# First rows of x loaded untransposed and interleaved with the blocks of wkA, five warm-ups for seven, in a gated pair of linear-attention blocks

## The chip, the cores and the metric

One core of a Trainium2 chip. The metric is the device time of one execution in microseconds (us). The kernel before takes 185.69 us, the median of three runs (185.13 to 186.56).

## The reference

Two linear-attention blocks A and B work on the same x, and a gate made from x mixes their outputs. S is 2048 rows, D is 640, with 32 heads of 20; all tensors are bf16.

```python
def block(x, wqkv, wo):
    q, k, v = heads(x @ wqkv)                      # 32 heads of 20
    phi = lambda t: where(t > 0, t + 1, exp(t)) + 1e-6
    pq, pk = phi(q), phi(k)
    kv  = einsum("bhsd,bhse->bhde", pk, v)
    z   = pk.sum over s
    num = einsum("bhqd,bhde->bhqe", pq, kv)
    den = einsum("bhqd,bhd->bhq", pq, z) + 1e-6
    return merge(num / den) @ wo

g = sigmoid((x * gate_w).sum(-1))
out = g * block(x, A_wqkv, A_wo) + (1 - g) * block(x, B_wqkv, B_wo)
```

## The kernel before

TensorE (PE) multiplies matrices, VectorE (DVE) and ScalarE (ACT) do the element-wise work out of PSUM, GpSimd (POOL) sets up small constants, and SyncE (SP) and ACT issue transfers, each on a queue of its own. In the parts under `manual_schedule`, `k_first` among them, the order of instructions on each engine is the order of the code; elsewhere a scheduler places them.

Work on the 2048 rows goes in 16 chunks of 128. A chunk of k is made by ten products (`k_mm`, L220): five blocks c of the inner dimension 640, and two halves hf of the 640 outputs. The left side is the transposed x (`xT`, five blocks of 128 by 2048), the right side the k part of the weights (`wkA`, five blocks). A 321st column in the second half of block A's weights holds `gate_w`, so that the same products give the gate's logit. `k_done` then makes `phi`: exp on ACT (L207), the logit's copy on ACT (L226), two steps on DVE (L212, L216).

`xT` has two sources. Rows 0 to 255 are loaded as they are into `xn` (L116) and transposed on PE against the identity (`x_transpose`, L199, five transposes per 128 rows), then copied from PSUM by DVE (L202). The other rows come by transposing loads on SP's queue (`x_turned`, L119): rows 256 to 511 first, then three times 512 rows. The loads of the start stand on two queues: SP has x's block 0, wkA's blocks 0, 2 and 4, the transposing load of rows 256 to 511, the whole of wqA (L132), and the other transposing loads; ACT has `gate_w`, x's block 1, and wkA's blocks 1 and 3.

While they are under way PE runs seven warm-up products on constants (L159), each 128x512, whose result is used by nobody. Then it turns `gate_w` into a column (L161), DVE copies the column, and POOL spreads it over wkA's extra column (L165). `k_first` transposes x's blocks 0 and 1, does the products of chunks 0 and 1 on blocks 0 to 2 in turn, then blocks 3 and 4, and then chunks 2 and 3 as wholes.

After that the first q products follow (`q_block` L278, `q_single` L288): for 512 rows at a time, with wqA as the left side. `q_block` fills two PSUM banks, one after the other, each with the five blocks c. PSUM has four slots of two banks (`ps`), which go round in a fixed order: chunks 0 to 3 have slots 2, 3, 0 and 1, and the first `q_block` has slot 2 again, so it waits until DVE is done with chunk 0. Later parts of the kernel are k, q, the sums over rows (Strassen products, L347), the same for block B, and at the end the output products (L570), which are added up by DVE (L575) and stored (L589).

Transfers carry one of eight semaphores in rotation, in the order of the code over both queues. A transfer waits until the one that had its semaphore before has landed. After its last transfer SP works down a list of waits, one for each semaphore, in the order 3 and 2, 4 and 1, 5 and 0, 6, 7, and then the program ends.

Of the kernel before, what the change touches and what calls it, by code (L numbers as in the profile page):

```python
# [8 lines left out]
P = 128  # L9
FP32 = mybir.dt.float32  # L10
BF16 = mybir.dt.bfloat16
# [3 lines left out]
S, D, H = 2048, 640, 32  # L15
Dh = D // H
DT = D // P
ST = S // P
NB = 4
CB = 4  # L20
HB = 512
# [10 lines left out]
def kernel(  # L32
# [11 lines left out]
    nc = tc.nc  # L44
# [6 lines left out]
    work = ctx.enter_context(tc.tile_pool(name="work", bufs=2))  # L51
# [6 lines left out]
    def ps_raw(name, slot=None):  # L58

        if slot is None:  # L60
            slot = turn[0]
            turn[0] = (slot + 1) % 4
        return psum.tile([P, 4 * HB], BF16, tag=f"ps{slot}", name=name)

    def ps(name, slot=None):

        return ps_raw(name, slot).bitcast(FP32).rearrange("p (b n) -> p b n", b=2)

    xT = persist.tile([P, DT, S], BF16, name="xT")
# [6 lines left out]
    ident = persist.tile([P, P], BF16, name="ident")  # L76
# [27 lines left out]
    wq_dram = [A_wqkv.rearrange("(c p) f -> p c f", p=P), B_wqkv.rearrange("(c p) f -> p c f", p=P)]  # L104
# [6 lines left out]
    wk = [None, None]  # L111
    wv = [None, None]
    wq = [None, None]
    wk[0] = wpool.tile([P, DT, D + 16], BF16, tag="wk", name="wkA")
    def load_x(eng, i):
        eng.dma_start(out=xn[:, i, :], in_=x2[i * P:(i + 1) * P, :])  # L116

    def x_turned(lo, hi):
        nc.sync.dma_start_transpose(out=xT[:, :, lo:hi], in_=x2[lo:hi, :])  # L119

    def load_wk(eng, lo, hi):
        eng.dma_start(out=wk[0][:, lo:hi, 0:D], in_=wq_dram[0][:, lo:hi, D:2 * D])

    grow = R[0][0:DT, 0:P]
    nc.scalar.dma_start(out=grow, in_=gate_w.rearrange("(c p) -> c p", p=P))
    load_x(nc.sync, 0)
    load_x(nc.scalar, 1)
    for c, eng in enumerate((nc.sync, nc.scalar, nc.sync, nc.scalar, nc.sync)):
        load_wk(eng, c, c + 1)
    x_turned(2 * P, HB)  # L130
    wq[0] = wpool.tile([P, DT, D], BF16, tag="wq", name="wqA")
    nc.sync.dma_start(out=wq[0][:], in_=wq_dram[0][:, :, 0:D])  # L132
    for n in range(1, NB):
        x_turned(n * HB, (n + 1) * HB)


    make_identity(nc, ident[:])
# [4 lines left out]
    for sign, base in ((1, 0), (-1, Dh - 1)):  # L142
        nc.gpsimd.affine_select(
            out=maskE[:], in_=maskE[:], pattern=[[-sign * Dh, WB[0] // Dh], [0, Dh]],
# [3 lines left out]
    for sign, base in ((1, 0), (-1, TW - 1)):  # L148
        nc.gpsimd.affine_select(
            out=headE[:], in_=headE[:], pattern=[[-sign * TW, H]],  # L150
# [4 lines left out]
    raw = ps_raw("warm", 3)  # L155
    warm = raw.bitcast(FP32).rearrange("p (b n) -> p b n", b=2)
    one_l, one_r = [nc.const_aps.tensor(1.0, [P, n], BF16) for n in (P, HB)]
    for k in range(7):
        nc.tensor.matmul(warm[:, 0, :], lhsT=one_l, rhs=one_r, start=True, stop=True)  # L159
    gcol = raw[:, 2 * HB:2 * HB + DT]  # L160
    nc.tensor.transpose(out=gcol, in_=grow, identity=ident[0:DT, 0:DT])  # L161
    gsb = work.tile([P, DT], BF16, tag="rT", name="gsb")
    nc.vector.tensor_copy(out=gsb[:], in_=gcol)
    for c in range(DT):
        nc.gpsimd.tensor_copy(out=wk[0][:, c, D:D + 1], in_=gsb[:, c:c + 1])  # L165

    def by_group(dst, lhsT, src, h):

# [28 lines left out]
    def x_transpose(i, pt, cuts=(0, DT)):  # L197
        for c in range(DT):
            nc.tensor.transpose(out=pt[:, c * P:(c + 1) * P], in_=xn[:, i, c * P:(c + 1) * P], identity=ident[:])  # L199
        src = pt[:, 0:D].rearrange("p (c n) -> p c n", c=DT)  # L200
        for lo, hi in zip(cuts, cuts[1:]):
            nc.vector.tensor_copy(out=xT[:, lo:hi, i * P:(i + 1) * P], in_=src[:, lo:hi])  # L202

    def phi(dst, src, n, lifted=False, side=None):

        e = work.tile([P, src.shape[1], n], BF16, tag="e", name="e", bufs=3)
        nc.scalar.activation(out=e[:], in_=src, func=ACT.Exp)  # L207
        if side is not None:
            side()
        if lifted:  # L210
            nc.scalar.activation(out=dst, in_=src, func=ACT.Identity, bias=lift[:])
        nc.vector.tensor_scalar(e[:], e[:], 1.0, EPS, op0=ALU.min, op1=ALU.add)  # L212
        if lifted:
            nc.vector.tensor_tensor(out=dst, in0=dst, in1=e[:], op=ALU.max)
            return
        nc.vector.scalar_tensor_tensor(out=dst, in0=src, scalar=1.0 + EPS, in1=e[:], op0=ALU.add, op1=ALU.max)  # L216

    def k_mm(b, i, c, pt, hf):
        w = HF + (hf if b == 0 else 0)
        nc.tensor.matmul(  # L220
            pt[:, hf, 0:w], lhsT=xT[:, c, i * P:(i + 1) * P], rhs=wk[b][:, c, hf * HF:hf * HF + w],
            start=(c == 0), stop=(c == DT - 1),
        )

    def k_done(b, i, pt):
        side = (lambda: nc.scalar.copy(out=logit[:, i:i + 1], in_=pt[:, 1, HF:HF + 1])) if b == 0 else None  # L226
        phi(pk[:, i, :].rearrange("p (b n) -> p b n", b=2), pt[:, :, 0:HF], HF, side=side)

    def k_chunk(b, i, slot=None):
        pt = ps(f"k{'AB'[b]}", slot)  # L230
        for hf in range(2):
            for c in range(DT):
                k_mm(b, i, c, pt, hf)
        k_done(b, i, pt)

    def k_first():

        pts = [ps("kA", 2 + i) for i in range(2)]
        raw = [ps_raw("xt", i) for i in range(2)]
        for i in range(2):  # L240
            x_transpose(i, raw[i], (0, 2, DT))

        def part(i, cs):
            for c in cs:
                for hf in range(2):
                    k_mm(0, i, c, pts[i], hf)

        for c in range(3):
            for i in range(2):
                part(i, (c,))  # L250
        for i in range(2):
            part(i, (3, 4))
            k_done(0, i, pts[i])
        for i in range(2, CB):
            k_chunk(0, i, i - 2)

    def mixed(t, m):

        return t[:, m::DT]
# [13 lines left out]
    def q_block(b, m, n):  # L273

        pt = ps(f"q{'AB'[b]}")
        for u in range(2):
            for c in range(DT):
                nc.tensor.matmul(  # L278
                    pt[:, u, :], lhsT=mixed(wq[b][:, c, :], m + u), rhs=xT[:, c, n * HB:(n + 1) * HB],
                    start=(c == 0), stop=(c == DT - 1),  # L280
                )
        phi(pqT[b][:, m:m + 2, n * HB:(n + 1) * HB], pt, HB)

    def q_single(b, m, n):
# [67 lines left out]
    def g_strassen(b, rT):  # L352
# [30 lines left out]
        if b == 0:  # L383
            wq[1] = load_w(1, "q", nc.scalar)
# [143 lines left out]
    part = [slice(n * RB, (n + 1) * RB) for n in range(4)]  # L528
# [113 lines left out]
                out_add(self.rows(0)[:, HF + lo:HF + hi], dst, self.v[:, lo:hi])  # L642
            self.store(0, HF if self.last else 0, D)

    def load_w(b, which, eng):
        lo = {"q": 0, "k": D, "v": 2 * D}[which]
        t = wpool.tile([P, DT, D], BF16, tag="w" + which, name=f"w{which}{'AB'[b]}")
        eng.dma_start(out=t[:], in_=wq_dram[b][:, :, lo:lo + D])
        return t

    def load_wo(b, eng):
        t = wo_sb[b] = wpool.tile([P, NW, D], BF16, tag="wo", name=f"wo{'AB'[b]}")
        for hf in range(2):
            for i, n in ((0, 2), (2, 1)):
                w, d0 = WB[i], hf * HF + i * WB[0]
                eng.dma_start(
                    out=t[:w, 3 * hf + i:3 * hf + i + n, :],
                    in_=wo_dram[b][d0:d0 + n * w, :].rearrange("(j p) f -> p j f", p=w),
                )
# [14 lines left out]


    with tc.manual_schedule():
        k_first()
    turn[0] = 2
    for n in range(2):
        for i in range(CB if n else 0, CB * 2 * n):  # L680
            k_chunk(0, i)
        for m in (0, 2):
            q_block(0, m, n)
        q_single(0, DT - 1, n)
    for i in range(hc, ST - 2):
        k_chunk(0, i)
    for n in range(NB):
        lo, hi = max(n * CB, 2), (n + 1) * CB
        nc.sync.dma_start(
            out=xn[:, lo:hi, :], in_=x2[lo * P:hi * P, :].rearrange("(q p) d -> p q d", p=P)  # L690
        )
    wv[0] = load_w(0, "v", nc.sync)
    load_wo(0, nc.sync)
    wk[1] = load_w(1, "k", nc.sync)

    def late_pool(name):
        return tc.tile_pool(name=name, bufs=1, space=bass.MemoryType.PSUM, reuse_waits="tile")
# [4 lines left out]
    with tc.manual_schedule():  # L702
# [17 lines left out]
        t = wpool.tile([P, 2, hc, HF], BF16, tag="wo", name="T13")  # L720
# [7 lines left out]
        t = wpool.tile([P, 2, DT, HF], BF16, tag="wq", name="TM12")  # L728
# [67 lines left out]
        for i in range(half - 1):  # L796
            p, after = pairs[i:i + 2]
# [45 lines left out]
```

## Time and profile before

| What | Value |
|---|---|
| median of three runs | 185.69 us |
| profiled execution | 186.37 us |
| its span, first to last instruction | 184.6 us |
| PE busy | 180.3 us, 98% of the span |
| DVE busy | 149.8 us, 81% |
| ACT busy | 75.1 us, 41% |
| bytes moved | 19.17 MB, mean 104 GB/s |

How to read it: "busy" counts the time in which an engine has an instruction at work; an L and a number is a line of the kernel. The span leaves out 1.77 us of the profiled execution that lie around the first and the last instruction. The chain of waits is followed back from the last instruction, at each step to what released it. A timeline line gives start, length, engine, line, operation, output <- inputs, sizes and count, and in brackets the idle time of the engine before it and what ended this. SPq and ACTq are the instructions that issue transfers. PE's matmuls are pipelined, so the sum of lengths can be longer than the time from the first to the last.

### The profile page before, as it was taken

What the parts mean: (1) busy time and instruction counts of PE and PEld (TensorE: products, weight loads), DVE (VectorE), ACT (ScalarE), POOL (GpSimd) and SP (SyncE); (2) the same over time, 40 slices, a digit from 0 to 9 for tenths busy, and PEclk for the clock granted to TensorE, in tenths of its full rate; (3) what the DMA queues carried; (4) which work ended last, traced back from release to release, by engine and by line L of the source; (5) the groups of instructions that cost most, each with busy time, mean ns of one, the idle gap of its engine ahead of it and who ended that gap; (6) DMA issues with size and microseconds to landing.
All of it is one profiled execution on the core that took longest, in us unless ns stands there. A gap on an engine that the chain in (4) does not pass through costs nothing.

```text
span 184.6 us, 3335 instructions
## 1 busy us (share of the span) xinstructions
PE 180.3 (98%) x1317; PEld 121.2 (66%) x1317; DVE 149.8 (81%) x239; ACT 75.1 (41%) x128; POOL 3.3 (2%) x22
## 2 busy tenths in 40 slices
PE   8999999999999999999999999999999999999993
PEld 3565757765567777877775555577778777777772
DVE  0286868889999999778788999779799999877873
ACT  2055545547962101357674577531102863111010
POOL 6000000000000000000000000000000000000000
PEclk9999999999999999999999999999999999999999
DMA  5999999124100270241115000000234570133333
GB/s 148 245 262 178 275 377 263 37 34 147 57 0 4 85 234 4 42 169 37 55 33 196 9 0 0 0 4 14 91 118 99 154 201 4 37 108 107 110 108 107
DMA packets 22518, 19.17 MB, mean 104 GB/s; under 512 B 10214, under 2 KB 21734, under 8 KB 22502
## 3 DMA queue, kind: packets, MB, share of 16 engines
q1 hardware_dynamic: 20564, 16.82, 33.6%
q10 hardware_dynamic: 1938, 2.13, 3.6%
q8 instruction: 10, 0.16, 0.4%
q14 instruction: 6, 0.05, 0.1%
HBM read 12.13 MB, written 4.53 MB: 90 GB/s over the span
## 4 chain that ended last, share of the span: by engine, by line
PE 94%; DMA 3%; ACTq 1%; DVE 0%; issue 0%
PE gs L347 17%; PE ox L570 12%; PE kB L220 12%; PE qB L267 12%; PE kA L220 12%; PE qA L267 6%; PE oz L570 6%; PE qA L278 5%; DMA wkA<-in_A_wqkv_dram 3%; PE gB L319 2%; PE gA L319 2%; PE ow L570 2%; PE qA L288 1%; PE s L474 1%; PE mA L474 1%; PE kvA L444 1%
## 5 line engine op out<-in xcount | busy, mean ns | idle before, releaser
L220 PEld LDWEIGHTS <-xT 128*128 128x128 bf16 x320 | 31.3, 98 | 13.2 <-issue 0.6
L212 DVE TENSOR_SCALAR e<-e 128x640 bf16<-128x640 bf16 (+2 forms) x53 | 19.0, 358 | 10.9 <-ACT e L207 9.7
L220 PE MATMUL kA<-wkA,xT 128*128 128x320 bf16 (+1 forms) x160 | 23.1, 304 | 0.2 <-DMA wkA<-in_A_wqkv_dram 0.2
L220 PE MATMUL kB<-wkB,xT 128*128 128x320 bf16 x160 | 23.0, 299 | 0.0
L267 PE MATMUL qB<-xT,wqB 128*128 128x512 bf16 x100 | 21.8, 379 | 0.0
L207 ACT ACTIVATE e<-kB 128x640 bf16<-128x640 f32 x16 | 11.3, 703 | 18.8 <-PE kB L220 18.8
L267 PEld LDWEIGHTS <-wqB 128*128 128x128 bf16 x100 | 11.7, 117 | 9.8 <-issue 0.2
L207 ACT ACTIVATE e<-kA 128x640 bf16<-128x640 f32 x16 | 11.2, 705 | 13.5 <-PE kA L220 13.5
L216 DVE SCALAR_TENSOR_TENSOR pk<-kA,e 128x640 bf16<-128x640 f32 x16 | 13.2, 825 | 2.1 <-DVE e L212 0.2
L216 DVE SCALAR_TENSOR_TENSOR pk<-kB,e 128x640 bf16<-128x640 f32 x16 | 13.2, 825 | 1.7
L207 ACT ACTIVATE e<-qB 128x1024 bf16<-128x1024 f32 x10 | 10.2, 1023 | 8.7 <-PE qB L267 8.3
L207 ACT ACTIVATE e<-qA 128x1024 bf16<-128x1024 f32 (+1 forms) x11 | 10.4, 946 | 8.1 <-PE qA L278 5.1
L347 PEld LDWEIGHTS <-xn 128*128 128x128 bf16 x96 | 9.2, 98 | 3.9 <-issue 0.4
L347 PEld LDWEIGHTS <-S 128*128 128x128 bf16 x96 | 9.4, 98 | 3.6
L620 ACT COPY u<-ox 128x320 f32<-128x320 f32 x8 | 3.4, 425 | 20.5 <-PE ox L570 20.5
L267 PE MATMUL qA<-xT,wqA 128*128 128x512 bf16 x50 | 11.0, 379 | 0.0
L570 PEld LDWEIGHTS <-xT 128*128 128x128 bf16 x85 | 8.1, 98 | 2.9
L570 PEld LDWEIGHTS <-pqTB 128*128 128x128 bf16 x80 | 7.8, 98 | 3.2
L570 PEld LDWEIGHTS <-pqTA 128*128 128x128 bf16 x80 | 7.7, 98 | 3.0
L347 PE MATMUL gs<-pk,xn 128*128 128x320 bf16 x64 | 9.4, 299 | 0.0
L216 DVE SCALAR_TENSOR_TENSOR pqTB<-qB,e 128x1024 bf16<-128x1024 f32 x7 | 8.6, 1225 | 0.7
L267 PEld LDWEIGHTS <-wqA 128*128 128x128 bf16 x50 | 5.9, 117 | 4.8
(126 smaller groups left out, 278.6 us busy)
## 6 DMA issues: line engine op xcount, KB each, us to landing
out_dram<-pk SPq DMA_DIRECT2D x14, 160.0 KB, 1.9
xn<-in_A_x_dram SPq DMA_DIRECT2D x3, 640.0 KB, 5.2
wqA<-in_A_wqkv_dram SPq DMA_DIRECT2D x1, 800.0 KB, 7.0
wvA<-in_A_wqkv_dram SPq DMA_DIRECT2D x1, 800.0 KB, 10.0
wkB<-in_B_wqkv_dram SPq DMA_DIRECT2D x1, 800.0 KB, 4.8
wqB<-in_B_wqkv_dram ACTq DMA_DIRECT2D x1, 800.0 KB, 5.2
wvB<-in_B_wqkv_dram SPq DMA_DIRECT2D x1, 800.0 KB
MA<-mA_dram SPq DMA_DIRECT2D x1, 800.0 KB, 4.2
```

What stands on the lines that cost most here:

```text
L207: nc.scalar.activation(out=e[:], in_=src, func=ACT.Exp)
L212: nc.vector.tensor_scalar(e[:], e[:], 1.0, EPS, op0=ALU.min, op1=ALU.add)
L216: nc.vector.scalar_tensor_tensor(out=dst, in0=src, scalar=1.0 + EPS, in1=e[:], op0=ALU.add, op1=ALU.max)
L220: nc.tensor.matmul(pt[:, hf, 0:w], lhsT=xT[:, c, i * P:(i + 1) * P], rhs=wk[b][:, c, hf * HF:hf * HF + w], start=(c == 0), stop=(c == DT - 1),
L267: nc.tensor.matmul(pt[:, u, :], lhsT=mixed(wq[b][:, c, :], m), rhs=xT[:, c, n * HB:(n + 1) * HB], start=(c == 0), stop=(c == DT - 1),)
L278: nc.tensor.matmul(pt[:, u, :], lhsT=mixed(wq[b][:, c, :], m + u), rhs=xT[:, c, n * HB:(n + 1) * HB], start=(c == 0), stop=(c == DT - 1),)
L288: nc.tensor.matmul(pt[:, 0, :], lhsT=mixed(wq[b][:, c, :], m), rhs=xT[:, c, n * HB:(n + 1) * HB], start=(c == 0), stop=(c == DT - 1),)
L319: nc.tensor.matmul(pt[:, hf, 0:HF], lhsT=xn[:, i, c * P:(c + 1) * P], rhs=pk[:, i, hf * HF:(hf + 1) * HF], start=(i == 0), stop=(i == ST - 1),
L347: nc.tensor.matmul(pt[:, n, 0:HF], lhsT=left[:, i, n * P:(n + 1) * P], rhs=right[:, i, :], start=(first and i == 0), stop=(i == hc - 1), s ...
L474: nc.tensor.matmul(dst[:w, 0:HF], lhsT=KVA[:w, k, 0:w], rhs=wo_sb[b][:w, k, n * HF:(n + 1) * HF], start=True, stop=True,)
L570: nc.tensor.matmul(dst, lhsT=left[:, c, r0:r0 + P], rhs=right[:, c, :], start=(first and c == 0), stop=(c == DT - 1), skip_group_check=not ...
L620: nc.scalar.copy(out=self.u6[:], in_=self.at("x"))
```

## The change

The first four blocks of x (rows 0 to 511) are now all loaded untransposed and turned on PE; the transposing load of rows 256 to 511 is gone, and so is the later load of these two blocks into `xn`. The loads of the start stand in a new order: ACT has x's block 1 first and `gate_w` after it; SP has everything else, the blocks of x and of wkA in turn. wqA comes in three pieces, wvA and wkB in two each.

On PE, five warm-ups are left, and the column of the gate is made between the transposes of x's blocks 0 and 1, with ACT and not DVE copying it. `k_first` then has: chunks 0 and 1 on wkA's blocks 0 and 1; transposes of x's block 2; chunks 0 and 1 on wkA's block 2; chunk 2 on blocks 0 to 2; transposes of x's block 3; blocks 3 and 4 for chunks 0, 1 and 2, each with its `phi`; chunk 3 as a whole. Inside a part the half hf is now the outer loop. `q_block` runs over the blocks c outside and the two banks inside. There are six more transfers on SP and two fewer on ACT, so the rotation of semaphores shifts by four: the last store has number 7 and not number 3, and the three stores before it have 6, 5 and 4 and not 2, 1 and 0.

```diff
-    nc.scalar.dma_start(out=grow, in_=gate_w.rearrange("(c p) -> c p", p=P))
-    load_x(nc.sync, 0)
-    load_x(nc.scalar, 1)
-    for c, eng in enumerate((nc.sync, nc.scalar, nc.sync, nc.scalar, nc.sync)):
-        load_wk(eng, c, c + 1)
-    x_turned(2 * P, HB)
     wq[0] = wpool.tile([P, DT, D], BF16, tag="wq", name="wqA")
-    nc.sync.dma_start(out=wq[0][:], in_=wq_dram[0][:, :, 0:D])
-    for n in range(1, NB):
-        x_turned(n * HB, (n + 1) * HB)
+
+    def first_loads():
+
+        load_x(nc.sync, 0)
+        load_x(nc.scalar, 1)
+        nc.scalar.dma_start(out=grow, in_=gate_w.rearrange("(c p) -> c p", p=P))
+        load_wk(nc.sync, 0, 1)
+        load_wk(nc.sync, 1, 2)
+        load_x(nc.sync, 2)
+        load_wk(nc.sync, 2, 3)
+        load_wk(nc.sync, 3, 4)
+        load_x(nc.sync, 3)
+        load_wk(nc.sync, 4, DT)
+        for lo, hi in ((0, 2), (2, 4), (4, DT)):
+            nc.sync.dma_start(out=wq[0][:, lo:hi, :], in_=wq_dram[0][:, lo:hi, 0:D])
+        for n in range(1, NB):
+            x_turned(n * HB, (n + 1) * HB)
...
-    for k in range(7):
-        nc.tensor.matmul(warm[:, 0, :], lhsT=one_l, rhs=one_r, start=True, stop=True)
-    gcol = raw[:, 2 * HB:2 * HB + DT]
-    nc.tensor.transpose(out=gcol, in_=grow, identity=ident[0:DT, 0:DT])
-    gsb = work.tile([P, DT], BF16, tag="rT", name="gsb")
-    nc.vector.tensor_copy(out=gsb[:], in_=gcol)
-    for c in range(DT):
-        nc.gpsimd.tensor_copy(out=wk[0][:, c, D:D + 1], in_=gsb[:, c:c + 1])
+
+    def warm_up(n, w):
+
+        for k in range(n):
+            nc.tensor.matmul(warm[:, 0, 0:w], lhsT=one_l, rhs=one_r[:, 0:w], start=True, stop=True)
+
+    def gate_column():
+
+        gcol = raw[:, 2 * HB:2 * HB + DT]
+        nc.tensor.transpose(out=gcol, in_=grow, identity=ident[0:DT, 0:DT])
+        gsb = work.tile([P, DT], BF16, tag="rT", name="gsb")
+        nc.scalar.copy(out=gsb[:], in_=gcol)
+        for c in range(DT):
+            nc.gpsimd.tensor_copy(out=wk[0][:, c, D:D + 1], in_=gsb[:, c:c + 1])
...
     def k_first():
 
-        pts = [ps("kA", 2 + i) for i in range(2)]
-        raw = [ps_raw("xt", i) for i in range(2)]
+        pts = {}
+
+        def part(i, cs, hfs=(0, 1)):
+            for hf in hfs:
+                for c in cs:
+                    k_mm(0, i, c, pts[i], hf)
+
+        warm_up(5, HB)
+        xt = [ps_raw("xt", 1), ps_raw("xt", 0)]
+        x_transpose(0, xt[0], (0, 2, DT))
+        gate_column()
+        x_transpose(1, xt[1], (0, 2, DT))
         for i in range(2):
-            x_transpose(i, raw[i], (0, 2, DT))
-
-        def part(i, cs):
-            for c in cs:
-                for hf in range(2):
-                    k_mm(0, i, c, pts[i], hf)
-
-        for c in range(3):
-            for i in range(2):
-                part(i, (c,))
+            pts[i] = ps("kA", 2 + i)
+            part(i, (0, 1))
+        late = ps_raw("xt", 1)
+        x_transpose(2, late, (0, DT))
+        pts[2] = ps("kA", 0)
         for i in range(2):
+            part(i, (2,))
+        part(2, (0, 1, 2))
+        x_transpose(3, late[:, 2 * HB:], (0, DT))
+        for i in range(3):
             part(i, (3, 4))
             k_done(0, i, pts[i])
-        for i in range(2, CB):
-            k_chunk(0, i, i - 2)
+        pts[3] = ps("kA", 1)
+        part(3, range(DT))
+        k_done(0, 3, pts[3])
...
-        for u in range(2):
-            for c in range(DT):
+        for c, u in [(c, u) for c in range(DT) for u in range(2)]:
...
-    for n in range(NB):
-        lo, hi = max(n * CB, 2), (n + 1) * CB
+    for n in range(1, NB):
+        lo, hi = n * CB, (n + 1) * CB
...
-    wv[0] = load_w(0, "v", nc.sync)
+    wv[0] = load_w(0, "v", nc.sync, (0, 3, DT))
     load_wo(0, nc.sync)
-    wk[1] = load_w(1, "k", nc.sync)
+    wk[1] = load_w(1, "k", nc.sync, (0, 3, DT))
```

## The prediction

> **What bounds the kernel now.** I read the engine shares first, then the chain of waits in order of time, then the timeline of the first 12 us, then the time of landing of the loads, and last the end of the span. The shares:
>
> ```profile
> span 184.6 us, 3335 instructions
> PE   8999999999999999999999999999999999999993
> ```
>
> TensorE (PE) is busy in every slice from the second to the last but one. The chain says where this packed stretch begins:
>
> ```profile
> 1.81 5.14 DMA wkA<-in_A_wqkv_dram
> 6.95 0.04 issue
> 6.99 5.07 PE kA L220 x36
> 12.05 4.32 PE qA L278 x20
> 16.37 1.08 PE qA L288 x5
> 17.45 5.45 PE kA L220 x40
> ...
> 180.13 0.76 PE ox L570 x5
> ```
>
> Columns: start, length, what. From 6.99 us the chain is PE alone to the end. What stands ahead of it is one transfer, block 1 of wkA, issued on ACT's queue at 1.81 and waited for until 6.95. So the change can gain only by bringing forward the start of the qA products (12.05), or after the last product. The head in detail:
>
> ```profile
> 0.84 3.15 PE L159 MATMUL warm<-const-bfloat16-1.0 128*128 128x512 bf16 x7 [0.84 <-PEq L827]
> 4.03 0.71 PE L199 MATMUL xt<-ident,xn 128*128 128x128 bf16 x5
> 4.79 0.56 DVE L202 COPY xT<-xt 128x256 bf16<-128x256 bf16 x2 [0.48 <-PE xt L199]
> 4.94 0.72 PE L199 MATMUL xt<-ident,xn 128*128 128x128 bf16 x5 [0.20 <-DMA xn<-in_A_x_dram]
> 5.45 1.31 PE L220 MATMUL kA<-wkA,xT 128*128 128x320 bf16 x4
> 6.99 5.07 PE L220 MATMUL kA<-wkA,xT 128*128 128x320 bf16 x36 [0.23 <-DMA wkA<-in_A_wqkv_dram]
> ```
>
> Two things are to be seen. First, only four kA products run before 6.99, in 1.31 us with their drain and a wait of some 0.3 us for a copy; two of them that follow each other start 0.27 us apart. The 36 after 6.99 are 5.07/36 = 0.14 apart. The page calls the granted clock full throughout, yet the same product costs twice as much before some point between 6.3 (start of the fourth) and 6.99. I call this point the switch. Warm-ups too are slow: 3.15/7 = 0.45 each. Second, the ten transposes cost PE about 0.5 us for five (4.94 to 5.45).
>
> **The change part by part.** Durations are from this execution, 186.37 us: a span of 184.6 and 1.77 around it. It lies 0.68 above the median of 185.69, so I carry differences over to the median.
>
> Removed: two warm-ups (2 x 0.43 = 0.86 us). The transposes of x's first block could then start at 3.06 instead of 4.03. They also need the block's landing. The issue (0.81) to landing row gives 2.2 us, hence 3.0; but block 1 of x is now first on the other queue and shares the engines. From
>
> ```profile
> GB/s 0 0 0 61 261 207 259 200 284 361 336 309 198 61 107 289 281 251 361 364 346 273 52 247 290 291 246 146 159 257 289 291 193 104 109 28 190 290 291 291
> ```
>
> (slices of 0.5 us from the start of the span) the sum of moved bytes is 264 KB at 3.0, 394 at 3.5, 492 at 4.0, 636 at 4.5, 816 at 5.0 and 984 at 5.5. Each block of x or wkA is 164 KB. In the new order two blocks of x are in at 3.3, wkA's block 0 at 4.0, block 1 at 4.6, x's block 2 at 5.0, wkA's 2 at 5.5. After that I take 289 to 300 GB/s, since the transposing load that falls into the slices of 198, 61 and 107 is gone: wkA's 3 at 6.0, x's 3 at 6.6, wkA's 4 at 7.1. I add 0.1 to 0.3 for the semaphore.
>
> Added: ten more transposes of x (blocks 2 and 3), 1.0 us of PE at the slow rate; two copies of 640 elements on DVE. The two copies there now, of 256 and 384 elements, take 0.29 and 0.35, which makes about 0.46 for 640.
>
> Moved: the products, interleaved. My schedule for PE: transposes of block 0 from 3.3 to 3.8, gate column to 3.9, transposes of block 1 to 4.4. The column's copy is now on ACT, and POOL spreads it at 0.18 a block by 4.8, so the second halves of the products wait little. Chunk 0, four products on wkA's 0 and 1: at 4.4, 4.7 (landing), 4.97, 5.24, so until 5.5. Chunk 1, four at 0.27: until 6.6. If the switch comes where it did, between 6.3 and 6.99, the rest is nearly all fast: transposes of block 2 0.45 (between the slow 0.5 and the half of it, nearer the slow), four products 0.55, a wait of 0.1 for DVE's copy, six products 0.82, transposes of block 3 0.4, twelve products 1.63 and ten 1.36. The sum is 5.31, so qA starts at 11.9, against 12.05: a gain of 0.15. The eight early products gain nothing to speak of, because they run slow and the ten new transposes take back what the wait for wkA gave.
>
> The last landing, 7.1 to 7.4, is well ahead of the products that need it (9.0): even at 229 GB/s, the mean from 3.0 to 4.0, the nine blocks of 1475 KB need 6.4 us from 1.8, so 8.2. The three loads of wqA end near 10 (819 KB more at 290), the first third near 8.4, ahead of 11.9; so cutting wqA and turning q_block's loops outside in cost nothing, and the loads' cover, the rest of chunk 3, would have to shrink by 1.5 us before they mattered. The transposing load of rows 512 to 1023 moves at 11.5 to 14.5 now, for chunk 4 at 17.3; behind an earlier wqA it is no later, so it keeps 2 us.
>
> Waits that are new: qA takes the buffer of chunk 0. From chunk 0's first exp (8.82) to its last DVE write is 2.04 us, and 18 products (2.45) stand between chunk 0's end and qA, so about 0.2 us is to spare. SP's new waits (x's block 3 on x's block 1, wkA's 4 on x's 0, wqA on gate column and wkA) all end before SP gets there at 0.45 a transfer (3.5 to 5.8). The second half of wkB is one more issue, 0.4 us, in front of the gate's transfers, and SP idles there from 39.67 to 41.40.
>
> The end: the last store now sits on the semaphore that SP's closing list asks for last (number 7) instead of first (number 3). The list has four more waits behind the old place, all satisfied by then. No row shows one; gaps between SP's transfers that hold such a wait are 0.04 to 0.05 us, so 0.04 to 0.2 with nothing as the low end. I take 0.1.
>
> Sum: 0.15 + 0.1 = 0.25 earlier. 186.37 becomes 186.1 in that execution, and the median 185.69 becomes 185.4.
>
> **Weighed against the Trainium skill.** The rows show that full speed came after seven warm-ups, ten transposes and four products. The Trainium skill (TensorE: Matmul & The Clock Gate, Part 4: PE-mode transpose) says that transposes do not engage the clock as products do; by it, a start with fewer warm-ups and more transposes keeps the half rate longer, which is the slower rival below. The ten transposes of this trace, in the 2.9 us before the switch, speak against it in part.
>
> **The rivals.**
> Early switch. Dense work begins at 0.84 and the switch was seen at 6.3 to 6.99, once; the four slow products do not say that it always falls there, since the wait for wkA hid it. If it comes by 4.4, the eight products run at 0.14: bound by landings, chunk 0 ends at 5.1 and chunk 1, waiting for DVE's copy, at 5.75; then transposes 0.4, copy wait 0.25, ten products 1.4, transposes 0.4, 22 products 3.0: 11.2. Gain 0.85 + 0.1, so 184.7. Against: this trace was still slow at 6.3. In its favour also stands a page's rule: the Trainium skill (TensorE: Matmul & The Clock Gate, Part 1) has a free-running window of 3.4 us, whose end can fall anywhere in such a stretch; by it the switch would move from run to run.
>
> Late switch, the slower case. Place: between the transposes of block 0 and block 1. x's block 1 landed at 4.94 now. If sharing keeps it or the gate column there, PE idles from 3.8 to 4.9 with nothing to warm it, where before a warm-up ran to 3.99. If the count then starts anew, it takes as long as from 0.84 to the switch, 5.5 to 6 us, so until 10.6. Everything to there runs slow: transposes to 5.4, eight products to 7.6, transposes to 8.1, four products to 9.2, six to 10.8, transposes to 11.2, 22 products fast to 14.2. Loss 2.1 - 0.1, so 187.7; with half that delay of the switch 186.7. It decides once PE is idle for about 1 us before its first kA product. Against: block 1 is now issued at 0.80 and not 1.41, with nothing ahead of it.
>
> Loads as the bound. 1475 KB instead of 1147 KB must land before chunk 0 can end. That binds only if wkA's last block lands after 8.9. It would take 1475 KB in 7.1 us, 208 GB/s throughout; at 180 it lands at 10.0 and qA starts at 13.0, so 186.5. No stretch of the first 6 us outside the transposing load was that slow for 1 us.
>
> The change not doing what it says: the head ends at 12.0 anyway and the end saves nothing, 185.7; this lies within my forecast.
>
> **How the numbers follow.** Forecast (185.4, its own range 184.9 to 185.9) 0.60; early switch 0.20; late switch 0.13; loads 0.05; other 0.02. The range goes from 184.3 (early switch with 0.2 at the end and landings 0.3 sooner) to 186.7 (late switch by half, or loads), leaving out the long late switch. One per cent is 1.86 us, which is about what a measurement of this kernel can tell from no change: its three runs lie within 1.43. Faster by more needs the early switch and 0.9 more than I find: 0.05. Slower by more needs the long late switch: 0.08. Within: 0.87.
>
> **What would show it.** Right: qA's first product at 11.7 to 12.1, chunk 0's first four products 0.27 apart, no wait of PE for wkA's last block, and the span ending 2.5 to 2.7 us after DVE's last write (2.67 now: 181.93 to 184.6). Wrong: kA products 0.27 apart after 7.0 (late switch), 0.14 apart before 6 (early), PE waiting over 0.3 us for a load after 7, or a stall at qA, whose buffer waits for DVE.

## The result, and the profile after

The changed kernel takes 186.94 us (median of nine executions, 186.21 to 187.59); the kernel before, run beside it, 185.44 (nine, 185.13 to 186.56). The ratio is 1.0074, with a 95% interval from 1.0054 to 1.0095 (below, intervals stand in brackets): slower by 0.74%, within the 1% that was forecast as the likeliest class, but above the range (184.3 to 186.7) and on the other side of the forecast of 185.4. Executions in which the clock fell back for a window (near 188.3 us, shown below) are left out of all ratios.

The profiled execution is the fastest of the nine, 186.21 us. Its chain of waits, in order of time (start, length, what):

```profile
0.81 2.73 DMA xn<-in_A_x_dram
3.54 0.05 issue
3.59 0.72 PE xt L213 x5
4.30 0.12 PE warm L175
4.42 0.65 PE xt L213 x5
5.06 1.98 PE kA L234 x8
7.04 0.28 PE xt L213 x5
7.32 0.55 PE kA L234 x4
7.86 0.04 issue
7.90 0.99 PE kA L234 x6
8.89 0.28 PE xt L213 x5
9.17 3.00 PE kA L234 x22
12.17 4.32 PE qA L301 x20
```

The one load still in the chain is x's block 0, and from 3.59 on PE is the chain. The wait for wkA's block 1 until 6.95 is gone, as the change says. Yet qA stands at 12.17 in this chain, 12.05 before: what the wait gave, the twenty transposes and the slow early products have taken. So the fastest execution of the changed kernel has the head of a slow execution of the kernel before. Why most are slower still is seen in a second execution of the same program, 187.70 us. PE's timeline of the head, first of the fastest, then of the second one (start, length, line, form, count):

```profile
3.59 0.72 PE L213 MATMUL xt<-ident,xn 128*128 128x128 bf16 x5 [0.45 <-DMA xn<-in_A_x_dram]
6.87 0.44 PE L213 MATMUL xt<-ident,xn 128*128 128x128 bf16 x5
7.15 1.74 PE L234 MATMUL kA<-wkA,xT 128*128 128x320 bf16 x10
8.73 0.44 PE L213 MATMUL xt<-ident,xn 128*128 128x128 bf16 x5
9.01 3.16 PE L234 MATMUL kA<-wkA,xT 128*128 128x320 bf16 x22
```

```profile
3.58 0.71 PE L213 MATMUL xt<-ident,xn 128*128 128x128 bf16 x5 [0.45 <-DMA xn<-in_A_x_dram]
4.85 2.65 PE L234 MATMUL kA<-wkA,xT 128*128 128x320 bf16 x8
7.29 0.74 PE L213 MATMUL xt<-ident,xn 128*128 128x128 bf16 x5
7.83 2.54 PE L234 MATMUL kA<-wkA,xT 128*128 128x320 bf16 x10
10.20 0.44 PE L213 MATMUL xt<-ident,xn 128*128 128x128 bf16 x5
10.48 3.16 PE L234 MATMUL kA<-wkA,xT 128*128 128x320 bf16 x22
```

The first transposes start the same to 0.01 us. In the chains qA is at 12.17 and at 13.64, 1.47 us later. The loads account for 0.2 of this: the second kA product waits for wkA's block 1 in both, until 5.27 in the first and until 5.46 in the second. The rest is the speed of PE: ten products of chunks 0 to 2 take 2.54 us here and 1.74 there, and five transposes 0.74 and 0.44. The clock's switch came at 6.63 in the first and at 9.88 in the second; both moments are the first entry of full clock in the trace's record of the granted clock. The PEclk row of the profile shows full clock in front of that entry too, where the products are at half speed: it has no record there.

In the traces the entries of that record are 3.413 us long or whole multiples of it (177.49 us is 52 of them), except the last, which the end of the program cuts off, and they begin anywhere relative to the program. Two traces, `after_w7f1` and `order_q`, have no entry; there only the distance of the products tells the clock. I call such a stretch of 3.413 us a window. The Trainium skill (TensorE: Matmul & The Clock Gate, Part 1) has a free-running window of about 3.4 us over which the gate watches how busy PE is. The entries of these traces agree with its length and with its free start.

### The profile page after: what moved, and what is told of

Its sections match the earlier page's. It is cut to its first block, busy times and chain, and to the rows that moved or that the text cites. A ratio compares the mean times of both kernels' runs of the same rounds, so it can differ in the third digit from the quotient of the medians.

```text
span 184.5 us, 3357 instructions
## 1 busy us (share of the span) xinstructions
PE 180.4 (98%) x1325; PEld 121.7 (66%) x1325; DVE 150.3 (81%) x240; ACT 75.1 (41%) x129; POOL 3.3 (2%) x22
## 4 chain that ended last, share of the span: by engine, by line
PE 96%; DMA 1%; DVE 0%; issue 0%
PE gs L370 17%; PE kA L234 12%; PE ox L593 12%; PE kB L234 12%; PE qB L291 12%; PE qA L291 6%; PE oz L593 6%; PE qA L301 5%; PE gB L342 2%; PE gA L342 2%; PE ow L593 2%; DMA xn<-in_A_x_dram 1%; PE qA L311 1%; PE xt L213 1%; PE s L497 1%; PE mA L497 1%
## 5 line engine op out<-in xcount | busy, mean ns | idle before, releaser
L234 PE MATMUL kA<-wkA,xT 128*128 128x321 bf16 (+1 forms) x160 | 23.7, 306 | 0.0
```

Source lines behind the costliest of these rows:

```text
L234: nc.tensor.matmul(pt[:, hf, 0:w], lhsT=xT[:, c, i * P:(i + 1) * P], rhs=wk[b][:, c, hf * HF:hf * HF + w], start=(c == 0), stop=(c == DT - 1),
```

## The experiments

For each profile I worked out how much of each window PE was filled, from the starts of its products: 0.43 us for a warm-up, 0.27 for a kA product, 0.11 for a transpose and 0.05 for the gate's column at half speed, or less where the next one starts sooner. With the column at 0 or at 0.11 the shares below move by up to 0.02, so they are estimates.

**A second profile of each kernel, and the warm-ups exchanged.** The changed kernel as it is (`after_again`):

> The changed kernel as it is, for the profile of another execution. The one profiled so far took 186.21 us, the fastest of its nine, and its head ended (first qA product) at 12.0; the median was 186.94. Late-switch theory: most executions get the full PE clock only one stretch later, so a profile of 186.7 or more shows kA products 0.27 us apart beyond 7.0 us and qA starting at 12.5 to 13.5. Loads theory: products are 0.14 apart from 7 us on, and PE waits for a block of x or wkA in the head. Tail theory: the head is as in the first profile and the excess lies after the last product.

Profile 187.70 us, median of eight 186.88, first qA product at 13.48 (13.64 in the chain), products 0.27 apart until 9.88: the late switch, as its theory said. The loads have only the 0.2 us above, and the end is as in the first profile (2.45 us after DVE's last write in both).

The changed kernel with seven warm-ups (`after_w7`):

```diff
-        warm_up(5, HB)
+        warm_up(7, HB)
```

> The changed kernel with seven warm-ups again. Late-switch theory: PE has no gap ahead of the first transposes (0.45 us with five), the switch comes by 7 us in nearly all executions, and the time falls to 185.5 to 186.0, with less spread. Loads theory: the first transposes start 0.3 us later, at 3.9, and nothing else changes: 186.9 to 187.2.

Median 185.93 (185.51 to 186.50) beside 185.88 of the kernel before, ratio 1.0002 [0.9982, 1.0022]. The loss is gone and the spread is 1.0 us; against the 186.88 of `after_again`, with the same executions of the kernel before beside it, the two warm-ups are worth 0.95 us. The profiled execution (186.50, the slowest) switched at 6.80.

The kernel before with five (`before_w5`, `range(7)` to `range(5)`):

> The kernel before with five warm-ups. Late-switch theory: the two warm-ups are what the clock needed; the 36 products after the wait for wkA run partly slow, 0.5 to 1.5 us more: 185.9 to 187. Loads theory: all that the warm-ups fill is hidden behind the wait for wkA's block 1, so 185.4 as before.

The twelve go from 184.91 to 188.44, median 186.76. Its profile (186.96) had no wait for wkA's block 1 at all, 40 products in 7.50 us from 5.14, and the switch at 9.16. So with five the switch can be late in the kernel before too, where the prediction's forecast counted the two warm-ups only as time saved. That it costs this kernel time is not shown: the ratio is 1.0014 [0.9982, 1.0047], three of the twelve (184.91, 185.37, 185.46) are as fast as the faster executions with seven, and one profile can't tell how often the switch is late.

The kernel before as it is (`before_again`):

> The kernel before as it is, for the profile of another execution, since the one profiled took 186.37 us, 0.9 above the median of 185.44. Late-switch theory: a typical execution has the switch no later than 7 us, and it is the landing of wkA's block 1 that moves its head; qA starts near 11.2. If instead the head ends at 12.05 again, the 0.9 us lie elsewhere.

This missed: it was 188.59 us, with qA at 14.26 in the chain. The switch came at 4.16, but was lost again. Engine time in stretches of this execution (behind the stretch and its length come PE, its weight loads, DVE, ACT and POOL, each with a count; then the granted clock, the view's DMA column and GB/s; PE and the clock are what counts here):

```profile
6.00:7.00 1.00, 0.00 (x0) 0.00 (x0) 0.00 (x0) 0.00 (x0) 0.00 (x0) 1.00 2.11 73
7.60:9.00 1.40, 1.40 (x6) 0.78 (x6) 0.00 (x0) 0.00 (x0) 0.00 (x0) 0.50 0.88 215
9.00:10.90 1.90, 1.90 (x8) 1.05 (x7) 0.00 (x0) 0.00 (x0) 0.00 (x0) 0.50 1.08 335
11.00:12.00 1.00, 1.00 (x9) 0.73 (x8) 0.33 (x1) 1.00 (x3) 0.00 (x0) 1.00 1.22 291
```

PE has nothing from 6 to 7 (it waited 1.69 us for wkA's block 1, until 7.52). The window from 4.16 to 7.58 was filled to 0.31, and the next, to 10.99, ran at 0.50: PE is busy throughout, with six products in 1.4 us. So the kernel before has a fault of its own, a wait long enough to lose the clock.

**How many, or where.** Seven products in all, but two of them behind the transposes of block 1 (`after_w5f2`):

```diff
         x_transpose(1, xt[1], (0, 2, DT))
+        warm_up(2, HB)
```

> The changed kernel with five warm-ups at the start and two more products of the same kind behind the transposes of x's block 1, where PE otherwise waits for wkA's block 1: seven in all, but the gap of 0.45 us ahead of the first transposes stays. Window theory (the clock is granted at the end of a free-running window of 3.41 us that PE filled by more than some 0.72 to 0.75): the window that ends near 6.5 is filled by more than with five, so nearly all executions switch by 7; the price is what the two products delay, 0.2 to 0.4: 186.0 to 186.3, spread about 1 us. Count theory (the clock needs seven warm-ups in a row at the start): no better than the changed kernel, 186.9 to 187.2.

Both theories missed: 187.52, not 186.0 to 186.3 and not 186.9 to 187.2, with two executions at 185.84 and the others from 186.85 to 187.84. In the profile (187.84) the window from 2.77 to 6.18 was filled to 0.74 and not granted; the switch came at 9.59, and the two products had delayed the rest (first kA product at 5.74, with five alone at 4.86). So seven in all is not enough: with the gap ahead of the first transposes left open, this window was not filled enough.

Seven at the start and one there (`after_w7f1`):

> The changed kernel with seven warm-ups at the start and one behind the transposes of x's block 1. Window theory: PE is busy from 0.84 to 5.5 without a gap, so the switch falls between 3.4 and 6.8 in every execution, 5.1 on average: 185.3 to 185.8, and no execution above 186.6. Count theory: the eighth product adds nothing, so 185.9 to 186.2, as with seven.

186.03 (185.52 to 186.47), ratio 0.9986 [0.9963, 1.0009]. As expected no execution is over 186.6; the median is as the count theory had it. In its profile (186.21) the products go from 0.27 to 0.14 apart near 6.2, ahead of the 6.63 of the fastest execution with five; but the extra product holds the first kA product back to 5.50, and qA is at 12.17 in the chain, the same as there. The kernel before with nine (`before_w9`):

> The kernel before with nine warm-ups. Window theory: they run to 4.7, where the kernel with seven waits for x's block 1 anyway; fewer executions miss a window, so the upper half of the times goes: median 185.2 to 185.6, highest under 187. But a switch that comes early can be lost again while PE waits for wkA's block 1, which keeps some executions above 187. Count theory: 185.4 to 185.9, as with seven.

186.19 (185.30 to 186.55), ratio 0.9999 [0.9974, 1.0023]: the slow end is cut, as expected, but the median is not lower, and neither theory's range holds it. In the profile (185.69) the switch came at 3.91, wkA's block 1 at 6.26, and qA at 11.37, 0.7 sooner than in the execution that the prediction was made from, in which block 1 came at 6.95.

Three (`after_w3`) and six (`after_w6`) in the changed kernel:

> The changed kernel with three warm-ups. Window theory in the form that the runs have shaped: with five, no window that begins before about 3.1 us (the gap ahead of the first transposes) is filled enough, so the switch falls evenly between 6.5 and 9.9, whatever the first warm-ups do; with three it is the same windows: 186.9 as with five, lowest no lower than 186.1, highest near 187.8. Count theory (each warm-up brings the switch nearer by its own length): two fewer cost as much as the two before, 187.7 to 188.0.

> The changed kernel with six warm-ups: they end at 3.4, so the gap ahead of the first transposes shrinks from 0.45 to about 0.15 us, with no later start of these. Threshold reading of the windows (a step between five and seven, none between three and five): windows that begin between 0 and 3 now qualify in part; median between 185.9 (seven) and 186.9 (five), with both early and late executions in the twelve: 186.2 to 186.6. Rival (a smooth count): half way, 186.4, without a spread wider than 1.2 us.

Three: 187.18 (186.59 to 187.67), ratio 1.0061 [1.0036, 1.0086]; three cost no more than five do (1.0074). Six: 186.09, ratio 1.0012 [0.9982, 1.0041], eleven executions from 185.73 to 186.42 and one at 187.89. So there is a step between five and six, as the threshold reading has it; that eleven of twelve are fast is more than the mixture that I expected. Six end at 3.36, counted from their starts, and leave 0.28 us ahead of the first transposes (3.64); five leave 0.65.

How full must a window be for full clock to be granted at its end? Of the windows of all profiles those nearest to this bound are 0.71, 0.74, 0.74 and 0.75, which were not granted, and 0.74, 0.79, 0.82 and 0.83, which were. So the bound is near three quarters of a window, with 0.74 seen on both sides; it is worked out from these counts, and no run sets the filling by itself. With five warm-ups, by the same count, PE is dense from 0.84 to 2.94 and from 3.59 on, with 0.65 us of nothing between. A window that begins between 2 and 3.1 is then filled to 0.65 to 0.70 at half speed in `after_again`, to 0.59 to 0.66 in `after_third` below, and to 0.70 to 0.75 in the fastest execution, where wkA's block 1 came soonest. In the profiles with six and seven, which close the gap, the same windows have 0.83, and 0.84 to 0.92.

A third profile of the changed kernel (`after_third`) was to test whether the switch alone sets its time:

> A third profile of the changed kernel. Window theory: the head and the time follow from the moment of the switch alone. Between 6.63 (186.21 us) and 9.88 (187.70 us) it is 0.46 us per us of switch; so a switch at s gives 186.21 + 0.46 (s - 6.63) within 0.2, and s lies between 6.4 and 9.9. Rival (loads also move it): the time departs from this line by 0.4 or more, with PE waiting for a load after 6 us.

The switch came at 8.72; the line gives 187.17, and 187.21 was measured. The seventeen times of the two timed series run from 186.21 to 187.70 without a gap of more than 0.22, as switches spread up to 9.9 make them; that the windows fall evenly is concluded, not shown. The switch is not quite alone: in the profile of `after_w3` it came at 8.18, for which the line gives 186.92, and 187.15 was measured, with wkA's block 1 waited for until 5.70 and not 5.27.

**The end.** The kernel before with four more transfers late in the kernel (`before_tail`):

```diff
-    wv[0] = load_w(0, "v", nc.sync)
+    wv[0] = load_w(0, "v", nc.sync, (0, 2, 4, DT))
...
-    wk[1] = load_w(1, "k", nc.sync)
+    wk[1] = load_w(1, "k", nc.sync, (0, 2, 4, DT))
```

> The kernel before with wvA and wkB each loaded in three pieces: four more transfers, so that the last store has semaphore 7, and nothing else changes. The span's end after DVE's last write falls from 2.67 to 2.45 us, as in the profiles of the changed kernel, and the median by 0.2. Rival: the 0.2 us come from somewhere else in the changed kernel, and the end stays at 2.67.

185.90 beside 185.82, ratio 0.9993 [0.9969, 1.0016], too wide for the effect. The profiles are sharper. From DVE's last write to the end of the span it is 2.71 us in the four profiles with the last store on number 3 (2.705 to 2.715) and 2.44 to 2.46 in the twelve with number 7, this one among them. So the last part of the change gains 0.26 us. The traces show where it is: behind the landing of the last store SP has four closing waits left with number 3 and none with number 7, and the four, long satisfied, take 0.065 us each.

**What the rest of the change is worth.** The kernel before with wkA's blocks in order on one queue, x's block 1 first on the other, and the last store on number 7 by the cuts of `before_tail` (`before_order`; the diff shows the loads):

```diff
-    nc.scalar.dma_start(out=grow, in_=gate_w.rearrange("(c p) -> c p", p=P))
     load_x(nc.sync, 0)
     load_x(nc.scalar, 1)
-    for c, eng in enumerate((nc.sync, nc.scalar, nc.sync, nc.scalar, nc.sync)):
-        load_wk(eng, c, c + 1)
+    nc.scalar.dma_start(out=grow, in_=gate_w.rearrange("(c p) -> c p", p=P))
+    for c in range(DT):
+        load_wk(nc.sync, c, c + 1)
```

> The kernel before (seven warm-ups, rows 256 to 511 by the transposing load), with two edits: x's block 1 first on ACT and all five blocks of wkA on SP in their order ahead of the transposing load, and wvA and wkB in three pieces, so that the last store has semaphore 7. In the changed kernel's profiles wkA's block 1 landed at 5.2 to 5.6 instead of 6.3 to 7.5 on this order. Theory (the landing of block 1 sets the head of the kernel before, and the ten added transposes are what the changed kernel pays for its order): products start 1.2 us sooner, some run slow, qA starts near 11.3: 0.5 to 0.9 under the kernel before run beside it, 185.0 to 185.3. Rival: the transposing load, now behind wkA, lands after 9, chunk 2 waits for it, and nothing is gained: 185.6 to 186.2.

186.38, from 185.19 to 187.86, ratio 1.0022 [0.9990, 1.0055]: the theory missed for the median, and the rival's range lies below it too, though the profiled execution had qA at 11.12. A second profile (`before_order2`):

> A second profile of the kernel before with wkA in order, whose twelve times run from 185.19 (profiled, switch at 4.0, PE waiting 0.25 us for the transposing load) to 187.86. Two theories for the slow ones: the switch is late or is lost again (products 0.27 apart after 7), or the transposing load lands late (PE waits for it over 1 us ahead of chunk 2).

Neither. It took 186.69 us with an early switch (5.64) and no wait for chunk 2; PE's weight load waited ahead of qA for the single load of wqA, which landed at 12.43 (in `before_order` at 10.78):

```profile
12.47 0.80 PEld L278 LDWEIGHTS <-wqA 128*128 128x128 bf16 x5 [1.57 <-DMA wqA<-in_A_wqkv_dram]
```

The change has the remedy: wqA in pieces and the blocks c outermost. So `order_q` is `before_order` with the change's three pieces of wqA, its `q_block`, and its two pieces of wvA and wkB, that is, the change without the ten added transposes, the interleaved products and the new place of the gate's column, and with seven warm-ups:

> The change without its ten added transposes and with seven warm-ups: wkA in order on SP, gate weights after x's block 1, rows 256 to 511 still by the transposing load (as is the products' order in the first four chunks), wqA in three pieces with the blocks c outermost, wvA and wkB in two pieces, last store on semaphore 7. Theory: what is left of the change is worth the wait for wkA's block 1 (its landing at 5.2 to 5.6 and not 6.3 to 7.5) and 0.22 us at the end; the wait for the whole of wqA, seen in the second profile of the kernel with wkA in order, is gone: 185.0 to 185.5, 0.3 to 0.6% under the kernel before beside it. Rival: the transposing load ahead of wqA still delays its first piece, and the time is as with wqA whole, 186.0 to 186.5.

185.32 us beside 185.81, ratio 0.9965 [0.9944, 0.9987], with all twelve between 185.18 and 185.49, as its theory had it. It is 0.35% faster than the kernel before beside it and, by the ratios, than the changed kernel (1.0074). Its chain:

```profile
5.59 2.64 PE kA L221 x18
8.23 0.03 issue
8.27 2.90 PE kA L221 x20
11.17 4.32 PE qA L278 x20
```

The first 20 products are done by 8.2 and the other 20 follow the transposing load. Beside the changed kernel with seven warm-ups (1.0002) it is 0.0037 lower, some 0.7 us; both have the end at number 7 and the loads of wkA in order. It differs from it in the ten transposes, the order of products that goes with them, the transposing load in place of two blocks of x, and the gate's column, which the changed kernel makes later and copies on ACT; what each of these is worth was not tested.

Why an early switch need not help the changed kernel shows in `after_w6`, where it came at 5.72:

```profile
8.55 0.30 PE L234 MATMUL kA<-wkA,xT 128*128 128x320 bf16 x1
9.27 3.02 PE L234 MATMUL kA<-wkA,xT 128*128 128x320 bf16 x21 [0.42 <-DMA wkA<-in_A_wqkv_dram]
```

One product, then a wait for wkA's last block until 9.23; qA stands at 12.29. This landing varies: by the entries of its semaphore it came between 8.00 and 9.32 in the eight profiles of the changed kernel and its variants, at 8.06 in the fastest execution. So what an early switch is worth with an early landing is not shown.

## Why the prediction was wrong, point by point

**The step that failed** is the forecast's "If the switch comes where it did, between 6.3 and 6.99, the rest is nearly all fast". It took from one execution a moment that varies, and it took the two warm-ups as time that could be cut, when they held the clock's window above its bound. What the runs put in its place: with five, three profiles have it at 6.63, 8.72 and 9.88; with six and seven at 5.72 and 6.80. Of the error of 1.54 us (186.94 against 185.4) 0.73 is this, the distance of the median from the execution with the switch at 6.63; by the line above the median stands for a switch at 8.2. The experiment puts it somewhat higher: giving the two warm-ups back brought 0.95. The rest lies mostly in the start value.

**The start value.** The profiled execution of before had a switch at 6.78 and wkA's block 1 at 6.95, and took 186.37, 0.93 above the later median of 185.44. "I carry differences over to the median" was therefore wrong, although in terms of that execution the forecast of 186.1 met the one like it (186.21): the head of 12.05 was a slow one, and against a faster one (11.37 with block 1 at 6.26, seen with nine warm-ups) the changed kernel's 12.17, or 12.46 in the profile with seven, is a loss even with the switch in time. Seven warm-ups give 185.93 beside 185.88, with 0.26 us of it won back at the end.

**The late-switch rival** had the mechanism and the sign, at 0.13. Its point of decision was wrong: it asked for 1 us of idle PE, and 0.65 us between the last warm-up and the first transposes, counted from starts (0.45 in the timeline), was enough. Its prices, 186.7 for half the delay and 187.7 for the whole, are near the median (186.94) and the slow end (187.70). Its place was wrong too: not between block 0 and block 1 of x, but ahead of block 0, which landed at 3.54 and not at 3.3.

**The rule of the Trainium skill on transposes** (TensorE: Matmul & The Clock Gate, Part 4: PE-mode transpose) was set aside only in part, and the traces speak against it: by it transposes don't engage the clock. In the execution of before, the window from 3.36 to 6.78 was filled to 0.74, of which 0.30 were transposes, and was granted; 0.75 of warm-ups alone, in the first window of `after_w7`, was not. Without its transposes the granted window would be at 0.44. So here they count, and about as products do.

**The early-switch rival**, 184.7, did not come. No profile of the changed kernel or its variants has the switch by 4.4; the earliest is 5.72. Its sum had wkA's last block in by 7.1 to 7.4, worked out from sums of bytes; no profile has it before 8.00, and in `after_w6` it landed at 9.23. The rival of loads as the bound asked for a landing after 8.9, and there it was, at a lower price (9.27 less 8.55 less 0.14 for the product, some 0.6 us), since PE was not yet at that point before 8.7.

**The schedule for PE** held where the switch was as assumed: first kA product at 4.86 (said 4.4), 0.27 apart until 6.6, qA first at 12.01 (said 11.9), no wait of PE for wkA's last block, no stall ahead of qA. In part this was luck: products began 0.46 late, and the ten transposes, put at 0.85 us together, ran at full speed and took 0.56 in the chain. The gain of 0.15 in the head was none even on paper: the schedule adds up starts, 11.9, and compares with 12.05 of the chain, while by starts the first qA product of before is at 11.89.

**The end** was mis-sized: 0.1 (0.04 to 0.2) was taken, 0.26 measured. The gaps between transfers on SP, 0.04 to 0.05, were short of the 0.065 of a closing wait, and the low end of nothing had no ground.

Still open: why the kernel before, with nine warm-ups, is no faster in the median; why wkA's last block lands anywhere from 8.00 to 9.32; and the exact bound of the gate.

## What to carry to other kernels

A warm-up product whose result and time nobody needs can still be needed: look at what it does to the granted clock over the next window before counting it as free, and profile more than one execution where the clock's window begins at a random place. A load that a later product needs in parts should come in parts, with the loop over the parts outermost; and a transposing load that is just in time can be better than transposes on the engine that bounds the kernel, as the fastest variant here suggests. A difference smaller than the spread of one kernel's own executions is not to be worked out from one profile.

## What the runs showed of the hardware that I had not expected

The clock can be lost by a wait that is shorter than a window: 1.69 us of idle PE within the window from 4.16 to 7.58 (filled to 0.31) cost a whole window at half clock, to 10.99, and 1.7 us (36 products in 6.74 us, not 5.07). The Trainium skill (TensorE: Matmul & The Clock Gate, Why this matters for your kernels) warns of idle gaps above about 3 us; this execution shows a shorter one doing it. And the order of the closing waits is worth 0.26 us, 0.065 us for each that is left behind the last store.
